# One MLP weight laid unevenly over the partitions, and part of it loaded early in small transfers

## The chip, the cores and the metric

The kernel runs on one core of a Trainium2 chip. The metric is the device time of one launch, in microseconds; the number for the kernel before is the median of three runs. Inside the launch, the profile's times count from the first instruction.

## The reference

One decode step of a transformer block whose norms are modulated by a condition vector. There is one token, D = 640, 32 heads of 192, a cache of 8192 positions, and an MLP of width 1536 with a squared ReLU. All is float32.

```python
mod = (silu(c) @ w_mod).reshape(1, 6, 1, -1)
sa, ca, ga, sb, cb, gb = (mod[:, i] for i in range(6))
h = layernorm(x) * (1 + ca) + sa
q = (h @ wq) per head
p = softmax(q . k_cache * 192 ** -0.5)
x = x + ga * ((p . v_cache) @ wo)
h = layernorm(x) * (1 + cb) + sb
h = relu(h @ w1 + b1)
x = x + gb * ((h * h) @ w2 + b2)
```

The caches are 2 x 32 x 8192 x 192 floats, about 403 MB, and every byte of them is read once.

## The kernel before

**Loads.** Everything big comes through one queue (SyncE, named SP), in the order in which the program writes the loads. A head has a load of keys (`load_k`, 48 KB per partition, and with them, for most heads, 7.5 KB of a query or output weight) and a load of values (`load_v`, 48 KB per partition). They go into a pool of three slots (`strm`, tag `slot`); a load waits on SP until its slot is free. All 128 partitions take part in each, with the same bytes. Behind head 31 come the weights of the tail, again through slots: `wm1` (last output weight and three modulation weights), `w1`, `gb`, and last `w2`, in the pieces of `W1_CUT` and `W2_CUT`.

**A head** (the loop over `h` near the end). `keys` multiplies the cached keys with the query on DVE (L201), adds the two halves of a part of the products on GpSimd (POOL, L203), and sums over the head dimension on DVE (L204, L205), in two halves of the positions, for the last head in four. `softmax` takes the maximum over partitions through TensorE (L220) and the exponential on ScalarE (L228). `values` multiplies with the cached values on TensorE (L240). `project` and `attend` turn a pair of heads into output rows a little later; `query` makes the next pair's query.

**The tail**, in this order: the last pair's `project` and `attend`, the second norm (with two modulation vectors made between its steps), the first MLP matmul `ps_f` (L343), bias, ReLU and square on DVE (L346 to L348), a transpose to columns (`fT`, L82), the last modulation vector (L140), two rounds of idle matmuls (L355), the second MLP matmul `ps_y` (L363), and two DVE operations (L366, L367) before the store of `y`.

**How the MLP lies on the partitions.** The 128 partitions are four groups of 32. The hidden width 1536 is cut into four parts of FG = 384, one per group, and each part into FB = 12 blocks of 32. The matmul `ps_f` therefore runs, for each of KB = 5 blocks of the input, four matmuls of 384 columns, one into each group's strip of output partitions. `fT` holds, per partition, one hidden element of each of the 12 blocks. `w2` is stored to match: each partition holds 12 rows of 640 floats, one per block, and `ps_y` runs 12 blocks of four matmuls of 160 columns over all 128 partitions. The load of `w2` is cut into pieces of 6, 3, 1, 1 and 1 blocks, and each piece's matmuls may start when it is there.

`spread` brings biases from columns to rows; its temporary tile and `f` share one buffer (tag `spread`).

Of the kernel before, what the change touches and what calls it, by code (L numbers as in the profile page):

```python
# [8 lines left out]
F32 = mybir.dt.float32  # L9
# [4 lines left out]
P = 128  # L14
D = 640
# [4 lines left out]
G = 4  # L20
DG = D // G
FG = FF // G
KB = DG // 32
FB = FG // 32
PW = 2 * DH
E = 8
ED = 64
# [9 lines left out]
WITHOUT_W = (1, H - 2)  # L37
WITH_W = tuple(h for h in range(H) if h not in WITHOUT_W)
W1_CUT = ((0, 3), (3, 2))
W2_CUT = ((0, 6), (6, 3), (9, 1), (10, 1), (11, 1))  # L40
WARM = 2
EPS = 1e-5


@with_exitstack
def block_kernel(ctx: ExitStack, tc: tile.TileContext, kw, ky, vc, wm0, wm1, w1, gb, w2, out):
    nc = tc.nc
    const = ctx.enter_context(tc.tile_pool(name="const", bufs=1))
    strm = ctx.enter_context(tc.tile_pool(name="strm", bufs=3))
    work = ctx.enter_context(tc.tile_pool(name="work", bufs=2))  # L50
# [3 lines left out]
    def slot(name):  # L54
        return strm.tile([P, SLOT], F32, tag="slot", name=name, bufs=3)
# [16 lines left out]
    wm0_t = slot("wm0_t")  # L72
    nc.sync.dma_start(wm0_t[:, :wm0.shape[1]], wm0)

    small = const.tile([P, 2 * KB + FB + KB], F32, name="small")
    nc.vector.tensor_copy(small, wm0_t[:, KB * 2 * D + WQ:wm0.shape[1]])  # L76
    x_c, c_c, bbc = small[:, :KB], small[:, KB:2 * KB], small[:, 2 * KB:]

    def columns(src, n, name, pool=const, **how):

        t = pool.tile([P, n // 32, 32], F32, name=name, **how)
        nc.vector.transpose(t.rearrange("p b r -> p (b r)"), src)  # L82
        return t

    def spread(src, n, name):

        t = work.tile([P, FB + KB, 32], F32, name=name + "_c", tag="spread", bufs=1)
        nc.vector.tensor_copy(t[:, :n], src[:, :, None].to_broadcast([P, n, 32]))
        r = const.tile([P, 32 * n], F32, name=name)
        nc.vector.transpose(r, t[:, :n].rearrange("p b r -> p (b r)"))  # L90
        return r
# [38 lines left out]
    mods = const.tile([P, 6, DG], F32, name="mods")  # L130
# [19 lines left out]
    def load(src, to, h, what):  # L150
        to[h] = slot(f"{what}{h}")
        n, w = CUTS.get((what, h), 1), src.shape[1]
        for c in range(n):
            a, b = c * HD // n, (c + 1) * HD // n if c + 1 < n else w
            nc.sync.dma_start(to[h][:, a:b], src[:, a:b])

    def load_k(h):

        load(kw[WITH_W.index(h)] if h in WITH_W else ky[WITHOUT_W.index(h)], k_t, h, "k")

    def load_v(h):
        load(vc[h], v_t, h, "v")
# [14 lines left out]
    def query(i, w):  # L177
        w = w.rearrange("p (b n) -> p b n", b=KB)
        ps = psum.tile([P, 512], F32, tag="q", name=f"ps_q{i}", bufs=2)
        for b in range(KB):  # L180
            nc.tensor.matmul(ps[:, :PW], hR[:, b], w[:, b], start=(b == 0), stop=(b == KB - 1))  # L181
        qb_t[i] = work.tile([P, PW], F32, name=f"qb{i}", tag="qb")
        nc.scalar.activation(qb_t[i], ps[:, :PW], AF.Copy, scale=DH ** -0.5)  # L183
# [27 lines left out]
    def inverse(i):  # L211
        r = work.tile([P, 2], F32, tag="r", name=f"r{i}")
        nc.vector.reciprocal(r, sum_t.pop(i))
        ri_t[i] = r
# [30 lines left out]
    def project(i):  # L245

        n = 32 * NV
        os_ = work.tile([P, 2, ED], F32, tag="os", name=f"os{i}")
        inverse(i)
        r2 = ri_t.pop(i)  # L250
        for a in range(2):
            h = 2 * i + a
            om = work.tile([P, ED, E], F32, tag="om", name=f"om{h}", bufs=1)
            nc.vector.scalar_tensor_tensor(om[:n], ps_t.pop(h)[:n].rearrange("p (d e) -> p d e", e=E), r2[:n, a:a + 1],  # L254
                                           mask[:n, None, :].to_broadcast([n, ED, E]), op0=ALU.mult, op1=ALU.mult)
            nc.vector.tensor_reduce(os_[:n, a], om[:n], axis=AX.X, op=ALU.add)  # L256
        os_t[i] = psum.tile([P, 512], F32, tag="sm", name=f"ps_oT{i}", bufs=2)
        nc.tensor.matmul(os_t[i][:, :n], os_[:n].rearrange("p a d -> p (a d)"), quad[:n], start=True, stop=True)

    def attend(i, w):  # L260
        oT = work.tile([P, 96], F32, tag="oT", name=f"oT{i}")
        nc.vector.tensor_copy(oT, os_t.pop(i)[:, :96])  # L262
        w = w.rearrange("p (j n) -> p j n", j=3)
        if i + 1 < NPAIR:
            for j in range(3):
                for g in range(2):
                    nc.tensor.matmul(att_a[32 * g:32 * (g + 1), :2 * DG], oT[:, 32 * j:32 * (j + 1)],  # L267
                                     w[:, j, 2 * DG * g:2 * DG * (g + 1)], start=(i == 0 and j == 0), stop=(i == NPAIR - 2 and j == 2))
            return
        for j in range(3):  # L270
            for g in range(G):
                nc.tensor.matmul(att_t[0][32 * g:32 * (g + 1), :DG], oT[:, 32 * j:32 * (j + 1)],
                                 w[:, j, DG * g:DG * (g + 1)], start=False, stop=(j == 2))

    def gather():

        nc.scalar.activation(att_s[:64], att_a[:64, :2 * DG], AF.Copy)
        att_t.append(psum.tile([P, 512], F32, tag="o", name="att", bufs=3))
        for g in range(G):
            nc.tensor.matmul(att_t[0][32 * g:32 * (g + 1), :DG], ident[:, 32 * (g // 2):32 * (g // 2) + 1].to_broadcast([P, 32]),  # L280
                             att_s[:, DG * (g % 2):DG * (g % 2 + 1)], start=True, stop=False)

    x_t = spread(x_c, KB, "x_t")
    bbt = spread(bbc, FB + KB, "bbt")
    for h in range(H):
        i = h // 2
        if h:
            load_k(h)
        if h == H - 1:
            wm1_t = slot("wm1_t")  # L290
            nc.sync.dma_start(wm1_t[:, :WO + KB * D], wm1[:, :WO + KB * D])
        load_v(h)
        w = k_t[h][:, HD:]

        def between(c):
            if c == 0 and h % 2 and i:
                attend(i - 1, w)
            elif c == 0 and h % 2 == 0 and i + 1 < NPAIR:
                query(i + 1, w)
            elif c == 2 and h == H - 1:  # L300
                gather()

        if h % 2 and i:
            project(i - 1)
        sc = keys(h, between)
        p = softmax(h, sc)
        if h == H - 1:
            next(mod(2, 1, wm1_t[:, WO:WO + KB * D].rearrange("p (b n) -> p b n", b=KB)))
        values(h, p)
# [3 lines left out]
    w1_t = slot("w1_t")  # L313
# [3 lines left out]
    w2_t = slot("w2_t")  # L317
    for b0, n in W2_CUT:
        nc.sync.dma_start(w2_t[:, b0 * D:(b0 + n) * D], w2[:, b0 * D:(b0 + n) * D])
    gb_t = w1_t[:, KB * FF:KB * (FF + D)].rearrange("p (b n) -> p b n", b=KB)  # L320
    w1_t = w1_t[:, :KB * FF].rearrange("p (b n) -> p b n", b=KB)
    w2_t = w2_t[:, :FB * D].rearrange("p (b n) -> p b n", b=FB)

    project(NPAIR - 1)
    attend(NPAIR - 1, wm1_t[:, :WO])
    mod_b = mod(3, 2, wm1_t[:, WO + KB * D:WO + KB * 3 * D].rearrange("p (b n) -> p b n", b=KB), (2, 2, 1))
# [11 lines left out]
    hT2 = columns(layernorm(x1, 32, scale_b, lambda: mods[:, 3], "ln2", lambda: next(mod_b)), DG, "hT2")  # L338

    pf = psum.tile([P, 512], F32, tag="q", name="ps_f", bufs=2)  # L340
    for b in range(KB):
        for g in range(G):
            nc.tensor.matmul(pf[32 * g:32 * (g + 1), :FG], hT2[:, b], w1_t[:, b, FG * g:FG * (g + 1)],  # L343
                             start=(b == 0), stop=(b == KB - 1))
    f = work.tile([P, FG], F32, name="f", tag="spread", bufs=1)
    nc.vector.tensor_add(f, pf[:, :FG], bbt[:, :FG])  # L346
    nc.vector.tensor_scalar(f, f, 0.0, None, op0=ALU.max)
    nc.vector.tensor_mul(f, f, f)  # L348
    fT = columns(f, FG, "fT", work, tag="om", bufs=1)

    next(mod(5, 1, gb_t))
    idle = psum.tile([P, 512], F32, tag="sm", name="ps_warm", bufs=2)
# [1 line left out]
        for g in range(G):  # L354
            nc.tensor.matmul(idle[32 * g:32 * (g + 1)], ones[:, :32], w1_t[:, k, :512], start=True, stop=True)  # L355
    gb2 = const.tile([P, DG], F32, name="gb2")
    nc.vector.tensor_mul(gb2, mods[:, 5], bbt[:, FG:])
    nc.vector.tensor_add(x1, x1, gb2)

    py = psum.tile([P, 512], F32, tag="q", name="ps_y", bufs=2)  # L360
    for b in range(FB):
        for g in range(G):
            nc.tensor.matmul(py[32 * g:32 * (g + 1), :DG], fT[:, b], w2_t[:, b, DG * g:DG * (g + 1)],  # L363
                             start=(b == 0), stop=(b == FB - 1))
    y = const.tile([P, DG], F32, name="y")
    nc.vector.tensor_mul(y, py[:, :DG], mods[:, 5])  # L366
    nc.vector.tensor_add(y, y, x1)  # L367
# [43 lines left out]
```

## Time and profile before

| | |
|---|---|
| median of three runs | 1057.88 us (1057.36 to 1058.01) |
| profiled execution, span | 1055.5 us |
| instructions | 5687 |
| DVE busy | 831.4 us (79%) |
| TensorE busy (PE) | 463.7 us (44%) |
| GpSimd busy (POOL) | 194.8 us (18%) |
| ScalarE busy (ACT) | 33.4 us (3%) |
| moved by DMA | 452.18 MB, mean 428 GB/s over the span |

The span runs from the first to the last instruction of the profiled execution; the median is 2.4 us above it, and that difference holds what lies around the instructions. A line such as "L201 DVE ... k<-k,qb" names the source line, the engine, the tile written and the tiles read. "Idle ... <-" is the time for which the engine stood still before the instruction, and what released it. "DMA share" is the mean busy share of the core's 16 DMA engines; q1 is the queue of the kernel's own loads, q8 and q14 bring instructions. The chain is followed back from the last instruction, at each step to what released it.

### The profile page before, as it was taken

To read this page: it belongs to the slowest core of one execution; us is meant where nothing else is said; L and a number is where in the kernel's file an instruction comes from. 1 tells how busy PE (TensorE), PEld (TensorE's weight loads), DVE (VectorE), ACT (ScalarE), POOL (GpSimd) and SP (SyncE) were. 2 spreads that over 40 slices of the span, in tenths; PEclk is the share of its full clock that TensorE was granted. 3 is DMA by queue.
4 is the path that set the end of the run, shared out by engine and by line. 5 is a ranking of instruction groups with operands and counts; after the bars stand their busy time and mean duration, and the time that the engine had idled before them with its cause. 6 is when DMAs were issued, how large, how long until landed. Compare 5 with 4: busy or idle time off the path is not lost.

```text
span 1055.5 us, 5687 instructions
## 1 busy us (share of the span) xinstructions
PE 463.7 (44%) x2356; PEld 155.0 (15%) x2356; DVE 831.4 (79%) x409; ACT 33.4 (3%) x88; POOL 194.8 (18%) x72
## 2 busy tenths in 40 slices
PE   3234443355543345463334534335453335535446
PEld 1101111111111111120111111101111111111113
DVE  2886878978787987878888687997878798789963
ACT  1000000000000000000000000000000000000000
POOL 0211112211212221212221212221221221122110
PEclk9667666766666766666676666666666666767769
DMA  9999999999999999999999999999999999999997
GB/s 403 435 434 428 432 440 427 441 424 437 433 433 428 440 424 441 424 439 427 431 437 437 422 442 430 428 439 426 439 429 433 428 438 433 434 427 432 424 426 310
DMA packets 11410, 452.18 MB, mean 428 GB/s; under 512 B 1269, under 2 KB 1273, under 8 KB 1785
## 3 DMA queue, kind: packets, MB, share of 16 engines
q1 hardware_dynamic: 11384, 451.83, 99.3%
q8 instruction: 18, 0.29, 0.1%
q14 instruction: 8, 0.06, 0.0%
HBM read 451.82 MB, written 0.00 MB: 428 GB/s over the span
## 4 chain that ended last, share of the span: by engine, by line
DMA 42%; DVE 39%; PE 17%; ACT 1%; issue 1%; SPq 0%; DVEq 0%; ACTq 0%
DMA k<-in_kw 36%; DVE k L201 21%; PE ps_o L240 14%; DVE sc L204 12%; DVE sc L205 5%; DMA k<-in_ky 3%; DMA w_t<-in_w 2%; PE ps_mx L220 1%; DMA wm_t<-in_wm 1%; ACT p L228 1%; PE ps_sum L97 1%; PE ps_mod L140 1%; PE ps_q L181 1%; DVE nm L222 0%; DVE mp L218 0%
## 5 line engine op out<-in xcount | busy, mean ns | idle before, releaser
L201 DVE TENSOR_TENSOR k<-k,qb 128x6144 f32<-128x6144 f32 (+1 forms) x66 | 419.7, 6359 | 141.6 <-DMA k<-in_kw 134.4
L203 POOL TENSOR_TENSOR k<-k 128x1344 f32<-128x1344 f32 (+1 forms) x66 | 194.1, 2941 | 820.9 <-DVE k L201 476.1
L240 PE MATMUL ps_o<-v,p 128*32 128x512 f32 x1536 | 290.4, 731 | 17.2 <-ACT p L228 17.2
L204 DVE TENSOR_REDUCE sc<-k 128x18 f32<-128x3456 f32 (+1 forms) x66 | 240.5, 3644 | 4.3
L220 PE MATMUL ps_mx<-ident,mp 128*128 128x128 f32 x64 | 25.5, 501 | 416.2 <-DVE mp L218 416.2
L240 PEld LDWEIGHTS ps_o<-v,p 128*32 128x32 f32 x1536 | 68.4, 131 | 215.4 <-issue 193.1
L267 PE MATMUL att_a<-k,oT 128*32 128x320 f32 x180 | 49.6, 720 | 114.2 <-DVE oT L262 113.1
L205 DVE TENSOR_REDUCE sc<-k 128x14 f32<-128x1344 f32 (+1 forms) x66 | 99.0, 1500 | 0.0
L220 PEld LDWEIGHTS ps_mx<-ident,mp 128*128 128x128 f32 x64 | 16.1, 312 | 442.8 <-DVE mp L218 421.0
L181 PE MATMUL ps_q<-k,hR 128*128 128x384 f32 x150 | 52.3, 496 | 0.0
L228 ACT ACTIVATE p<-sc,nm 128x256 f32<-128x256 f32 x32 | 16.2, 508 | 760.6 <-DVE nm L222 496.9
L267 PEld LDWEIGHTS att_a<-k,oT 128*32 128x32 f32 x180 | 13.7, 161 | 136.7 <-DVE oT L262 116.7
L222 DVE TENSOR_REDUCE nm<-ps_mx 128x1 f32<-128x128 f32 x32 | 9.3, 291 | 28.5 <-PE ps_mx L220 28.5
L181 PEld LDWEIGHTS ps_q<-k,hR 128*128 128x128 f32 x150 | 27.3, 190 | 27.9 <-issue 11.7
L254 DVE SCALAR_TENSOR_TENSOR om<-ps_o,r,mask 96x512 f32<-96x512 f32 x32 | 23.9, 747 | 6.5 <-PE ps_o L240 5.4
L256 DVE TENSOR_REDUCE os<-om 96x64 f32<-96x512 f32 x32 | 21.8, 682 | 1.1
L140 PE MATMUL ps_mod<-wm_t,silu 128*32 128x320 f32 (+1 forms) x120 | 11.7, 550 | 14.6 <-DVE silu L128 14.6
L97 PE MATMUL ps_sum<-sp,ones 128*128 128x2 f32 x32 | 9.4, 364 | 17.2 <-ACT p L228 17.2
L183 ACT ACTIVATE qb<-ps_q 128x384 f32<-128x384 f32 x16 | 7.9, 491 | 195.2 <-PE ps_q L181 195.2
L97 PEld LDWEIGHTS ps_sum<-sp,ones 128*128 128x128 f32 x32 | 8.0, 312 | 21.9 <-ACT p L228 21.9
L145 DVE COPY mods<-ps_mod 128x320 f32<-128x320 f32 (+1 forms) x4 | 1.6, 398 | 10.2 <-PE ps_mod L140 10.2
L76 DVE COPY small<-wm_t 128x27 f32<-128x27 f32 x1 | 0.2, 179 | 11.2 <-DMA wm_t<-in_wm 11.2
(77 smaller groups left out, 90.9 us busy)
## 6 DMA issues: line engine op xcount, KB each, us to landing
k<-in_kw SPq DMA_DIRECT2D x29, 7104.0 KB, 27.4
v<-in_vc SPq DMA_DIRECT2D x32, 6144.0 KB, 22.1
k<-in_ky SPq DMA_DIRECT2D x1, 6144.0 KB, 28.3
k<-in_ky SPq DMA_DIRECT2D x2, 3072.0 KB, 21.5
k<-in_kw SPq DMA_DIRECT2D x3, 1536.0 KB, 15.5
wm_t<-in_wm SPq DMA_DIRECT2D x1, 4173.5 KB, 12.7
wm_t<-in_wm SPq DMA_DIRECT2D x1, 3200.0 KB, 29.3
wm_t<-in_wm SPq DMA_DIRECT2D x1, 2560.0 KB, 18.2
```

What stands on the lines that cost most here:

```text
L97: nc.tensor.matmul(ps[:, :n], ones, src, start=True, stop=True)
L140: nc.tensor.matmul(ps[32 * g:32 * (g + 1), :n * DG], e[:, b:b + 1].to_broadcast([P, 32]), wb[:, :, DG * g:DG * (g + 1)], start=(b == 0), s ...
L181: nc.tensor.matmul(ps[:, :PW], hR[:, b], w[:, b], start=(b == 0), stop=(b == KB - 1))
L201: nc.vector.tensor_mul(pr, pr, q[:, None, :].to_broadcast([P, n, DH]))
L203: nc.gpsimd.tensor_add(half, half, pr[:, m:, DH // 2:])
L204: nc.vector.tensor_reduce(s[:, :m], pr[:, :m], axis=AX.X, op=ALU.add)
L205: nc.vector.tensor_reduce(s[:, m:], half, axis=AX.X, op=ALU.add)
L220: nc.tensor.matmul(ps[:, :P], mp.to_broadcast([P, P]), ident, start=True, stop=True)
L228: nc.scalar.activation(p, sc[:, :, None].to_broadcast([P, NPOS, 32 // E]), AF.Exp, bias=nm, accum_out=sp[:, h % 2:h % 2 + 1])
L240: nc.tensor.matmul(ps_t[h][32 * g:32 * (g + 1)], p[:, E * j:E * (j + 1)].rearrange("p e r -> p (e r)"), t[:, j, g], start=(j == 0), stop=( ...
L254: nc.vector.scalar_tensor_tensor(om[:n], ps_t.pop(h)[:n].rearrange("p (d e) -> p d e", e=E), r2[:n, a:a + 1], mask[:n, None, :].to_broadca ...
L267: nc.tensor.matmul(att_a[32 * g:32 * (g + 1), :2 * DG], oT[:, 32 * j:32 * (j + 1)], w[:, j, 2 * DG * g:2 * DG * (g + 1)], start=(i == 0 an ...
```

## The change

The four groups no longer hold equal parts of the hidden width. Groups 0 and 1 (partitions 0 to 63) hold 14 blocks of 32, groups 2 and 3 (partitions 64 to 127) hold 10. The sum is 1536 as before.

- The load `w2`, last in the program, has 10 blocks for all 128 partitions, in pieces of 5, 2, 1, 1 and 1.
- The four blocks that only partitions 0 to 63 have, 64 rows of 10,240 B, 655 KB in all, go into a tile of their own, `w2x_t`. They come in eight transfers of eight rows each, issued by SP behind the values' load of heads 8, 10, 12, 14, 16, 18, 20 and 22. One transfer takes every fourth of 32 consecutive partitions: rows r, r+4, ... r+28.
- `ps_f` has matmuls of 448, 448, 320 and 320 columns in place of four of 384.
- `f` is 448 wide. Its last 128 columns are zeroed on partitions 64 to 127 before the last `project`. The bias is added in two operations: 320 columns on all partitions, 128 columns on partitions 0 to 63. The ReLU, the square and the transpose are 448 wide.
- `ps_y` runs 14 blocks: first the four of `w2x_t`, over 64 partitions, then the ten of `w2`.
- The bias columns in the first load grow by two per partition.

```diff
-FB = FG // 32
+FB = 10
+FX = 4
+FT = FB + FX
+F0 = (0, 32 * FT, 64 * FT, 64 * FT + 32 * FB)
+FN = (32 * FT, 32 * FT, 32 * FB, 32 * FB)
...
-W2_CUT = ((0, 6), (6, 3), (9, 1), (10, 1), (11, 1))
+W2_CUT = ((0, 5), (5, 2), (7, 1), (8, 1), (9, 1))
+X_AT = {8 + 2 * r: (r % 4) + 32 * (r // 4) for r in range(8)}
...
+    w2x_t = const.tile([64, FX * D], F32, name="w2x_t")
     for h in range(H):
...
         load_v(h)
+        if h in X_AT:
+            r = X_AT[h]
+            top = 32 * (r // 32 + 1)
+            nc.sync.dma_start(w2x_t[r:top:4], w2x[r:top:4])
...
+    f = work.tile([P, 32 * FT], F32, name="f", tag="spread", bufs=1)
+    nc.vector.memset(f[64:, 32 * FB:], 0.0)
     project(NPAIR - 1)
...
-            nc.tensor.matmul(pf[32 * g:32 * (g + 1), :FG], hT2[:, b], w1_t[:, b, FG * g:FG * (g + 1)],
+            nc.tensor.matmul(pf[32 * g:32 * (g + 1), :FN[g]], hT2[:, b], w1_t[:, b, F0[g]:F0[g] + FN[g]],
                              start=(b == 0), stop=(b == KB - 1))
-    f = work.tile([P, FG], F32, name="f", tag="spread", bufs=1)
-    nc.vector.tensor_add(f, pf[:, :FG], bbt[:, :FG])
+    nc.vector.tensor_add(f[:, :32 * FB], pf[:, :32 * FB], bbt[:, :32 * FB])
+    nc.vector.tensor_add(f[:64, 32 * FB:], pf[:64, 32 * FB:32 * FT], bbt[:64, 32 * FB:32 * FT])
     nc.vector.tensor_scalar(f, f, 0.0, None, op0=ALU.max)
     nc.vector.tensor_mul(f, f, f)
-    fT = columns(f, FG, "fT", work, tag="om", bufs=1)
+    fT = columns(f, 32 * FT, "fT", work, tag="om", bufs=1)
...
+    w2x_b = w2x_t.rearrange("p (b n) -> p b n", b=FX)
+    for b in range(FX):
+        for g in range(G):
+            nc.tensor.matmul(py[32 * g:32 * (g + 1), :DG], fT[:64, FB + b], w2x_b[:, b, DG * g:DG * (g + 1)],
+                             start=(b == 0), stop=False)
     for b in range(FB):
         for g in range(G):
             nc.tensor.matmul(py[32 * g:32 * (g + 1), :DG], fT[:, b], w2_t[:, b, DG * g:DG * (g + 1)],
-                             start=(b == 0), stop=(b == FB - 1))
+                             start=False, stop=(b == FB - 1))
```

The arrays are laid out to match on the host: `w2` as [128, 10 x 640], `w2x` as [64, 4 x 640].

More of the change, by code (lines that the diff above doesn't have):

```diff
@@ L45, in block_kernel @@
 @with_exitstack
-def block_kernel(ctx: ExitStack, tc: tile.TileContext, kw, ky, vc, wm0, wm1, w1, gb, w2, out):
+def block_kernel(ctx: ExitStack, tc: tile.TileContext, kw, ky, vc, wm0, wm1, w1, gb, w2, w2x, out):
     nc = tc.nc
@@ L73, in block_kernel @@
     nc.sync.dma_start(wm0_t[:, :wm0.shape[1]], wm0)
-    small = const.tile([P, 2 * KB + FB + KB], F32, name="small")
+    small = const.tile([P, 2 * KB + FT + KB], F32, name="small")
     nc.vector.tensor_copy(small, wm0_t[:, KB * 2 * D + WQ:wm0.shape[1]])
@@ L85, in spread @@
     def spread(src, n, name):
-        t = work.tile([P, FB + KB, 32], F32, name=name + "_c", tag="spread", bufs=1)
+        t = work.tile([P, FT + KB, 32], F32, name=name + "_c", tag="spread", bufs=1)
         nc.vector.tensor_copy(t[:, :n], src[:, :, None].to_broadcast([P, n, 32]))
@@ L283, in block_kernel @@
     x_t = spread(x_c, KB, "x_t")
-    bbt = spread(bbc, FB + KB, "bbt")
+    bbt = spread(bbc, FT + KB, "bbt")
+    w2x_t = const.tile([64, FX * D], F32, name="w2x_t")
     for h in range(H):
@@ L356, in block_kernel @@
     gb2 = const.tile([P, DG], F32, name="gb2")
-    nc.vector.tensor_mul(gb2, mods[:, 5], bbt[:, FG:])
+    nc.vector.tensor_mul(gb2, mods[:, 5], bbt[:, 32 * FT:])
     nc.vector.tensor_add(x1, x1, gb2)
     py = psum.tile([P, 512], F32, tag="q", name="ps_y", bufs=2)
+    w2x_b = w2x_t.rearrange("p (b n) -> p b n", b=FX)
[3 more added lines that the diff above has]
+                             start=(b == 0), stop=False)
     for b in range(FB):
@@ L385, in column, with hidden @@
         return a(v).reshape(G, n, 32).transpose(0, 2, 1).reshape(P, n)
+    def hidden(v):
+        b = np.zeros((P, FT), np.float32)
+        for g in range(G):
+            b[32 * g:32 * (g + 1), :FN[g] // 32] = a(v)[F0[g]:F0[g] + FN[g]].reshape(-1, 32).T
+        return b
+    w2 = a(B_w2)
+    w2m = np.stack([w2[F0[g]:F0[g] + 32 * FB].reshape(FB, 32, D).transpose(1, 0, 2) for g in range(G)])
+    w2e = np.stack([w2[F0[g] + 32 * FB:F0[g] + 32 * FT].reshape(FX, 32, D).transpose(1, 0, 2) for g in range(2)])
     wq = a(A_wq).reshape(G, KB, 32, NPAIR, PW).transpose(3, 0, 2, 1, 4).reshape(NPAIR, P, WQ)
@@ L397 @@
         "wm0": np.concatenate([rows(wm[:, :2 * D], KB), wq[0], column(A_x, KB), column(c, KB),
-                               column(B_b1, FB), column(B_b2, KB)], axis=1),
+                               hidden(B_b1), column(B_b2, KB)], axis=1),
         "wm1": np.concatenate([wo[-1], rows(wm[:, 2 * D:3 * D], KB), rows(wm[:, 3 * D:5 * D], KB)], axis=1),
@@ L401 @@
         "gb": rows(wm[:, 5 * D:], KB),
-        "w2": rows(B_w2, FB),
+        "w2": np.ascontiguousarray(w2m.reshape(P, FB * D)),
+        "w2x": np.ascontiguousarray(w2e.reshape(64, FX * D)),
     }
```

## The prediction

> **What bounds the kernel now.** I read the page first, for the engines, the DMA line and the chain.
>
> ```profile
> span 1055.5 us, 5687 instructions
> DMA  9999999999999999999999999999999999999997
> q1 hardware_dynamic: 11384, 451.83, 99.3%
> q8 instruction: 18, 0.29, 0.1%
> DMA 42%; DVE 39%; PE 17%; ACT 1%; issue 1%; SPq 0%; DVEq 0%; ACTq 0%
> ```
>
> The loads fill the 16 DMA engines for the whole span, apart from the last slice. DVE has the second largest share of the chain. So for each stage I ask which of the two ends last. The chain in order of time answers that for the end of the program.
>
> ```profile
> 912.48 26.83 DMA k<-in_kw
> 939.40 6.57 DVE k L201
> 963.46 0.81 PE ps_mx L220 x2
> 964.50 6.56 DVE k L201
> 1022.94 7.32 PE ps_o L240 x48
> 1032.07 19.60 DMA w_t<-in_w
> 1051.71 0.52 PE ps_y L363 x8
> ```
>
> The keys of head 29 (L201 at 939.40) are the last work of DVE that waits for a load. From there up to the last values (L240 at 1022.94) the chain shows DVE at heads 29, 30 and 31, with little but a short PE step between heads. Windows of this stretch say the same (columns: window, length, busy PE, PEld, DVE, ACT, POOL, clock, DMA share, GB/s):
>
> ```profile
> 965.00:975.00 10.00, 9.13 (x50) 2.54 (x50) 9.90 (x3) 0.28 (x2) 3.06 (x1) 0.80 1.01 437
> 1005.00:1015.00 10.00, 0.00 (x0) 0.00 (x0) 9.93 (x6) 0.00 (x0) 1.93 (x2) 0.58 1.02 437
> ```
>
> DVE is busy for 9.9 of 10 us. What follows (last values, attention output, norm, MLP) hangs on it. There are thus two paths to the end. One is compute, started by the landing of head 29's keys. The other is w2 itself, whose last piece the chain names. They end close together, as the timeline of the tail shows:
>
> ```profile
> 1039.47 5.13 PE L343 MATMUL ps_f<-w_t,hT 128*32 128x384 f32 x40 [2.10 <-issue]
> 1044.38 1.57 PE L140 MATMUL ps_mod<-w_t,silu 128*32 128x160 f32 x40
> 1045.74 1.93 PE L355 MATMUL ps_warm<-w_t,ones 128*32 128x512 f32 x16
> 1046.23 0.58 DVE L82 STREAM_TRANSPOSE fT<-f 128x384 f32<-128x384 f32 x1
> 1047.46 3.16 PE L363 MATMUL ps_y<-w_t,fT 128*32 128x160 f32 x80
> 1050.92 0.48 PE L363 MATMUL ps_y<-w_t,fT 128*32 128x160 f32 x8 [0.31 <-DMA w_t<-in_w]
> 1051.71 0.48 PE L363 MATMUL ps_y<-w_t,fT 128*32 128x160 f32 x8 [0.31 <-DMA w_t<-in_w]
> ```
>
> From 1047.46 to 1052.19 PE idles only twice for 0.31 us on w2, so the wait that can be removed here is 0.6 us.
>
> **Are the 16 engines alike?** The change moves bytes from one half of the partitions to the other, so this decides. Windows at the end of the loads:
>
> ```profile
> 1046.00:1047.00 1.00, 1.00 (x12) 0.32 (x8) 0.96 (x3) 0.00 (x0) 0.00 (x0) 1.00 0.98 392
> 1047.00:1048.00 1.00, 1.00 (x25) 0.70 (x20) 0.67 (x3) 0.00 (x0) 0.00 (x0) 1.00 0.60 241
> 1048.00:1049.00 1.00, 1.00 (x39) 0.98 (x31) 0.00 (x0) 0.00 (x0) 0.00 (x0) 1.00 0.58 221
> 1049.00:1050.00 1.00, 0.98 (x31) 0.66 (x24) 0.00 (x0) 0.00 (x0) 0.00 (x0) 1.00 0.54 197
> 1049.80:1050.00 0.20, 0.20 (x12) 0.19 (x8) 0.00 (x0) 0.00 (x0) 0.00 (x0) 1.00 0.40 154
> 1051.20:1051.40 0.20, 0.20 (x8) 0.00 (x0) 0.00 (x0) 0.00 (x0) 0.00 (x0) 1.00 0.00 0
> ```
>
> They are not. The share stands at 0.60 to 0.54, which is nine engines of 16 (0.56). Seven are done by about 1047, the nine between 1049.8 and 1051.2. So every engine had the same bytes, seven are early by some 3 us, and nine are late, spread over at most 1.4 us. A cause shows in a window around one packet of the instruction queue, and in the window up to head 29's keys:
>
> ```profile
> q8 instruction: 1, 0.02, 6.0%
> DMA packets 8690, 405.69 MB, mean 432 GB/s; under 512 B 961, under 2 KB 961, under 8 KB 961
> q1 hardware_dynamic: 8669, 405.41, 100.0%
> q8 instruction: 14, 0.23, 0.1%
> ```
>
> The first line is from a window of 1.0 us: 6.0% of 16 us is 0.96 us of one engine for one block of instructions. Fourteen of the 18 have come by 939.4, so the unevenness is mostly there by head 29. At 100.0% no engine idles before that: what an engine is given on top delays everything behind it in its queue.
>
> **The change, part by part.**
>
> *The eight transfers of eight rows.* Each row has 4 x 640 x 4 = 10,240 B. An engine moves 432/16 = 27.0 GB/s, so a row takes 0.38 us. How eight rows fall on engines the trace of before does not show. The nearest row is the output, four rows:
>
> ```profile
> DMA packets 8, 0.00 MB, mean 1 GB/s; under 512 B 4, under 2 KB 8, under 8 KB 8
> ```
>
> This window holds only that store: four rows, four completion writes (under 512 B), so four engines with a row each. I take eight engines with a row each, the same eight each time: 8 x 0.38 = 3.03 us on each of them, all before head 23, none on the other eight. Only seven engines are early. Whichever eight they are, at least one is of the nine late ones, and DVE starts head 29 when the last engine has landed its part. That engine is now later by 3.03 us, less what it was ahead of the latest of the nine (0 to 1.4 us). So the keys of head 29 land later by 1.6 to 3.0 us. I take 2.4, the middle, and all compute behind 939.40 moves with it.
>
> [...]
>
> SP issues each transfer behind the values' load of its head, into a tile of its own, so it waits for no slot; the issue holds up only the next key load, which waits for its slot anyway. Cost taken: nothing; bound 0.1 us each, off the path while engines never run dry.
>
> *w2 shorter by two blocks, all 128 rows.* Every engine saves 8 x 2 x 2560 B = 40,960 B, or 1.52 us, in the tail. Late engines outside the eight end w2 1.5 us earlier; the eight end 1.5 us later net. What is worth having is only the 0.6 us of PE waits.
>
> *The first MLP matmul.* Groups of 448, 448, 320, 320 columns replace four of 384. The four sit in different column strips and run side by side, so the longest should set the pace: 5.13 x 448/384 = 5.98, that is +0.85 us. Below: 0, if the sum of columns (1536 as before) counts. I take +0.85. The next two PE groups (L140, L355) follow at once and move with it.
>
> *DVE between the matmuls.* Rows for 384 columns and 160 columns:
>
> ```profile
> 1044.65 0.56 DVE L346 TENSOR_TENSOR f<-ps_f,bbt 128x384 f32<-128x384 f32 x1 [5.29 <-PE ps_f L343]
> 1045.24 0.36 DVE L347 TENSOR_SCALAR f<-f 128x384 f32<-128x384 f32 x1
> 1045.64 0.56 DVE L348 TENSOR_TENSOR f<-f 128x384 f32<-128x384 f32 x1
> 1033.69 0.33 DVE L329 TENSOR_TENSOR x<-att,mods 128x160 f32<-128x160 f32 x1 [1.15 <-PE att L272]
> 1037.96 0.24 DVE L335 TENSOR_SCALAR cb<-mods 128x160 f32<-128x160 f32 x1
> ```
>
> An add costs 0.23/224 us, about 1.0 ns, per column. One add of 384 becomes one of 320 and one of 128: 0.49 + 0.30 against 0.56, +0.23. The clamp gains 64 columns at 0.5 ns (+0.03), the square and the transpose 64 at 1.0 ns each (+0.13). Sum +0.39. fT is then ready 0.85 + 0.39 = 1.24 us after its 1046.81, at 1048.05; ps_y started 0.65 us after fT, held by the warm-up, which began at 1045.74 and took 1.93. It now starts between 1047.46 + 0.85 = 1048.3 (the warm-up's shift) and 1048.05 + 0.65 = 1048.7. I take 1048.45, +1.0.
>
> *The second MLP matmul.* 14 blocks for 12, the extra ones on half of the rows. The same shape without waits is L140's, here with its mean:
>
> ```profile
> L140 PE MATMUL ps_mod<-w_t,silu 128*32 128x160 f32 x40 | 1.6, 299 | 0.0
> ```
>
> Its 40 are ten steps of four side by side, in 1.57 us: (1.57 - 0.30)/9 = 0.141 us a step. A block of w2 is two steps, 14 blocks take 27 x 0.141 + 0.30 = 4.1 us (4.4 at an undivided 1.57/5 a block), if w2 is there. They end at 1052.55 against 1052.19: +0.36 us. Bounds: 0, if the columns' sum counts (the first matmul then costs nothing), and +0.9, with 4.4 us and a slower clock in the first matmul.
>
> *Zeroing f's unused half, wider bias, two columns more in the first load.* The memset runs on DVE before it waits for the last values, and there is cover:
>
> ```profile
> L254 DVE SCALAR_TENSOR_TENSOR om<-ps_o,r,mask 96x512 f32<-96x512 f32 x32 | 23.9, 747 | 6.5 <-PE ps_o L240 5.4
> ```
>
> 5.4 us of idle DVE hide some 0.2 us, which would be the price without it. The bias work stands before the first keys land. Cost: nothing.
>
> **Sum.** Head 29's keys +2.4, tail +0.36, together +2.75 us. Is w2 late instead? Before, its last piece freed PE at 1051.71; an engine of the eight ends 1.5 us later, at 1053.2 or earlier, while compute now wants the last blocks at about 1052.5 + 2.4. So compute ends last and w2 is off the path. The profiled execution's span would be 1055.5 + 2.75 = 1058.2; it stands 2.4 us under the median of 1057.88, so the median should be 1060.6. Bounds of this case: 1.6 + 0 gives 1059.5, 3.0 + 0.9 gives 1061.8.
>
> **The rivals.** *Not slower.* The eight engines hold the seven early ones and one that is late only at the very end (four of 18 instruction blocks come behind head 29's keys). If at head 29 it is within half a microsecond or so of the early ones (the 3 to 4 us from them to the latest, less 3.03), the 3.03 us stay inside the others' lateness, the path moves by nothing, the PE waits of 0.6 us go, and the tail gives +0.36 or, if the matmul follows the sum of columns, 1047.46 + 0.39 + 4.1 = 1051.95, -0.24 us. Time 1057.6 to 1058.3. For it: the windows show lateness at the end only. Against: 14 of 18 blocks were there before. The point is that half microsecond.
>
> *The rows do not fall on eight engines but on all 16, by halves or in turn.* Then each gets 1.52 us, head 29's keys are 1.5 late, and the time is 1057.88 + 1.5 + 0.36 = 1059.8. Against: the four writes of the output.
>
> *All eight rows on one engine, the same each time.* 8 x 8 x 0.38 = 24 us on it, of which up to 3 are its lead: 1079 to 1082. The change would not do what it says. Against: again four writes for four rows.
>
> [...]
>
> **How the numbers follow.** The main case gets 0.72; not slower 0.14; all 16 engines 0.06; one engine 0.03; fixed price 0.03; 0.02 for something unseen that gains. About 0.2% (2.1 us, from 1057.88 to 1060.0) is what a measurement of this kernel can tell from no change. The main case lies at 1059.5 to 1061.8, so about a sixth of it (0.12) is within 0.2%. Slower: 0.60 + 0.03 + 0.03 = 0.66; within: 0.12 + 0.13 + 0.06 = 0.31; faster 0.03. The likeliest is the main case, 1060.6. Range: its bounds, and down to 1058.1 to take in most of the not-slower case: 1058.1 to 1061.9.
>
> **What would show it.** Right: DVE's first keys of head 29 start near 941.8 rather than 939.40, and L363 starts near 1050.9 and runs 14 blocks without a DMA wait; L343 takes near 6.0 us; the windows at the end show the two groups of engines closer together and one or more of the eight last. Wrong: L201 for head 29 at 939.4 to 939.9 (then no engine's lateness grew), or a chain that still ends in a wait for w2. [...]

## The result, and the profile after

The kernel after takes 1059.68 us (median of 20 runs, 1058.53 to 1060.37), the kernel before beside it 1057.7 us: 1.0019 times as long, 95% interval 1.0012 to 1.0025. It is slower by 2.0 us (1.3 to 2.6), where 2.75 was forecast. A difference of 0.2% lies inside the interval: the point, 0.19%, belongs to what the forecast called within 0.2% (chance 0.31), the upper part of the interval to slower by more (0.66).

The page of after, the lines that answer to those of before:

```profile
span 1057.4 us, 5730 instructions
DMA  9999999999999999999999999999999999999996
q1 hardware_dynamic: 11512, 451.83, 99.1%
q8 instruction: 18, 0.29, 0.1%
DMA 40%; DVE 39%; PE 19%; ACT 1%; issue 1%; DVEq 0%; ACTq 0%
```

The chain in order of time (start, length, what):

```profile
915.73 26.15 DMA k<-in_kw
941.98 6.57 DVE k L206
966.04 0.81 PE ps_mx L225 x2
967.08 6.56 DVE k L206
992.83 9.05 PE ps_o L245 x48
1026.20 7.66 PE ps_o L245 x48
1051.33 2.90 PE ps_y L380 x80
```

Head 29's keys start on DVE at 941.98, not 939.40: 2.58 us later. Head 30's keys follow at the same distance; from its values (`ps_o` at 992.83) on it is more, of which below. The chain no longer ends in a load of w2; it ends in the second MLP matmul, which waits for no load. The timeline of the tail:

```profile
1043.08 3.58 PE L355 MATMUL ps_f<-w_t,hT 128*32 128x448 f32 x38 [2.10 <-issue]
1046.46 0.57 PE L355 MATMUL ps_f<-w_t,hT 128*32 128x448 f32 x2
1047.10 0.49 DVE L357 TENSOR_TENSOR f<-ps_f,bbt 128x320 f32<-128x320 f32 x1 [4.12 <-PE ps_f L355]
1047.51 0.27 DVE L358 TENSOR_TENSOR f<-ps_f,bbt 64x128 f32<-64x128 f32 x1
1048.90 0.65 DVE L87 STREAM_TRANSPOSE fT<-f 128x448 f32<-128x448 f32 x1
1050.04 1.29 PE L376 MATMUL ps_y<-w2x_t,fT 64*32 64x160 f32 x32
1051.26 2.92 PE L380 MATMUL ps_y<-w_t,fT 128*32 128x160 f32 x80
```

ps_y ends at 1054.18, before at 1052.19: 1.99 us later, which is the whole loss (the spans differ by 1.9). The engines at the end of the loads, in windows as before:

```profile
1047.00:1048.00 1.00, 1.00 (x37) 1.00 (x34) 0.86 (x3) 0.00 (x0) 0.00 (x0) 1.00 1.00 387
1048.00:1049.00 1.00, 1.00 (x20) 0.71 (x16) 0.93 (x3) 0.00 (x0) 0.00 (x0) 1.00 0.68 266
1049.00:1050.00 1.00, 1.00 (x12) 0.14 (x2) 0.97 (x3) 0.00 (x0) 0.00 (x0) 1.00 0.31 123
1050.00:1051.00 1.00, 1.00 (x30) 0.91 (x32) 0.44 (x2) 0.00 (x0) 0.00 (x0) 1.00 0.25 88
```

The step at nine engines is gone. Most now finish within a microsecond or two of each other, but four (0.25) are later still. The layout did even out most of the engines. The last of them no longer hold up PE; what costs is that three engines are late at head 29 (their landings are below).

### The profile page after: what moved, and what is told of

The parts are those of the page before. It is cut to its first block, busy times and chain, and to the rows that moved or that the text cites. A ratio compares the mean times of both kernels' runs of the same rounds, so it can differ in the third digit from the quotient of the medians.

```text
span 1057.4 us, 5730 instructions
## 1 busy us (share of the span) xinstructions
PE 466.2 (44%) x2372; PEld 155.6 (15%) x2372; DVE 832.1 (79%) x411; ACT 33.4 (3%) x88; POOL 194.8 (18%) x72
## 4 chain that ended last, share of the span: by engine, by line
DMA 40%; DVE 39%; PE 19%; ACT 1%; issue 1%; DVEq 0%; ACTq 0%
DMA k<-in_kw 36%; DVE k L206 21%; PE ps_o L245 14%; DVE sc L209 12%; DVE sc L210 5%; DMA k<-in_ky 3%; PE ps_mx L225 1%; DMA wm_t<-in_wm 1%; PE ps_mod L145 1%; ACT p L233 1%; PE ps_sum L102 1%; PE ps_q L186 0%; DVE nm L227 0%; DVE mp L223 0%; PE ps_f L355 0%
## 5 line engine op out<-in xcount | busy, mean ns | idle before, releaser
L245 PE MATMUL ps_o<-v,p 128*32 128x512 f32 x1536 | 296.7, 744 | 17.2 <-ACT p L233 17.2
```

What stands on the lines that cost most here:

```text
L245: nc.tensor.matmul(ps_t[h][32 * g:32 * (g + 1)], p[:, E * j:E * (j + 1)].rearrange("p e r -> p (e r)"), t[:, j, g], start=(j == 0), stop=( ...
```

## The experiments

Each ran beside the kernel before, on the same chip. "Head 29" is the start of the first half of that head's keys on DVE (L201; 939.40 before). Where a diff takes out lines of the transfers, it is against the first of these kernels, the transfers alone; in the last three experiments it is against the kernel after. Lines that only make the tile and its array are left out, and `...` marks other cuts.

**The transfers alone** (the MLP and w2 as before).

```diff
+        if h in X_AT:
+            r = X_AT[h]
+            top = 32 * (r // 32 + 1)
+            nc.sync.dma_start(w2x_t[r:top:4], w2x[r:top:4])
```

> The kernel before, with only the eight transfers of eight rows added (655 KB into a tile that nothing reads; w2 and the MLP as before). Theory (the last of the eight engines to land a head's keys sets the pace): head 29's keys start on DVE near 942.0, as after the change, against 939.4, and the whole time is 2.3 to 3.0 us above the kernel before. Rival (the time of the change comes from the uneven MLP in the tail, the transfers are hidden): head 29 at 939.4 to 939.9 and the time within 0.5 us of before. Rival (only bytes count): +1.5 us.

1060.11 us, 1.0023 (1.0014 to 1.0032), 2.6 us over before's 1057.55. Head 29, on the timeline of DVE:

```profile
941.92 6.56 DVE L202 TENSOR_TENSOR k<-k,qb 128x6144 f32<-128x6144 f32 x1 [3.25 <-DMA k<-in_kw]
```

This is the change's delay at head 29, without its MLP: the transfers are not hidden. The end of the chain differs from that of after, though:

```profile
1035.52 18.52 DMA w_t<-in_w
1054.08 0.52 PE ps_y L369 x8
```

With w2 at its full length, its last piece frees PE at 1054.08, 2.37 us later than before. The late engines thus delay both paths, and here w2 is the one that ends last. The change shortens w2, which leaves the path through head 29. That the uneven MLP is not what costs is worked out below, from the timeline of after.

**The same bytes over all 16 engines.**

```diff
+            r, b = X_AT[h]
+            nc.sync.dma_start(w2x_t[r::4, b * D:(b + 1) * D], w2x[r::4, b * D:(b + 1) * D])
```

> The kernel before, with the same 655 KB added at the same eight heads, but over all 128 partitions: eight transfers of 32 rows of 2,560 B, two rows on each of 16 engines. Not read. Theory: each engine gets 1.5 us instead of eight getting 3.0, so head 29's keys start near 940.9 and the time is 1.3 to 1.7 us above before. Rival (a fixed price per transfer, wherever it goes): as much as the transfers to 64 partitions. Rival (hidden): 0 to 0.5.

1059.13 us, 1.0015 (1.0006 to 1.0024), 1.6 us; head 29:

```profile
941.19 6.56 DVE L202 TENSOR_TENSOR k<-k,qb 128x6144 f32<-128x6144 f32 x1 [3.24 <-DMA k<-in_kw]
```

That is 1.79 us, near the 1.5 of an even share. At most 0.3 us is left for a fixed price of all eight transfers.

**Twice over to partitions 0 to 63**, one transfer at each of heads 8 to 23.

```diff
-X_AT = {8 + 2 * r: (r % 4) + 32 * (r // 4) for r in range(8)}
+X_AT = {8 + r: (r % 4) + 32 * (r // 4 % 2) for r in range(16)}
```

> The kernel before, with the eight transfers of eight rows to partitions 0 to 63 made twice over, one at each of heads 8 to 23 (1.3 MB, not read). Theory: 6.1 us on each of the eight engines in place of 3.0, all of the second 3.0 unhidden: head 29's keys at 944.9 to 945.2, the time 5.4 to 5.9 us above before. Rival (a part is hidden, or the price is paid once): 2.5 to 4 us.

1062.84 us, 1.0050 (1.0035 to 1.0066), 5.2 us; head 29:

```profile
945.29 6.56 DVE L202 TENSOR_TENSOR k<-k,qb 128x6144 f32<-128x6144 f32 x1 [3.25 <-DMA k<-in_kw]
```

The time lies under the 5.4 to 5.9 of the theory and over the 2.5 to 4 of the rival; head 29, at 945.29, is just past the theory's 945.2. The second set adds 3.37 us to head 29 after the first added 2.52: the second pays in full (3.0 by bytes), the first had a little hidden. In time the second set costs no more than the first (5.2 is twice 2.6), so this run does not tell the theory from a price by bytes.

**Four rows instead of eight**, half the bytes.

```diff
-            nc.sync.dma_start(w2x_t[r:top:4], w2x[r:top:4])
+            nc.sync.dma_start(w2x_t[r:r + 16:4], w2x[r:r + 16:4])
```

> The kernel before, with eight transfers of four rows of 10,240 B (rows r, r+4, r+8, r+12; half of the bytes of the transfers-only run), not read. Theory (3.0 us on each of the four lowest of the eight engines): it depends on whether one of the three late ones is among the four. If so, head 29's keys at 941.9 to 942.1 and 2.2 to 2.8 us above before, as with twice the bytes; if not, head 29's keys at 939.4 to 940.0 and 0 to 0.7 us. Rival (bytes count): 0.7 us for four engines' share, or half of 2.6, 1.3 us, with head 29's keys near 940.7.

1059.39 us, 1.0016 (1.0007 to 1.0025), 1.5 us, less than the 2.2 foretold for this case; but head 29 agrees with it:

```profile
941.72 6.56 DVE L202 TENSOR_TENSOR k<-k,qb 128x6144 f32<-128x6144 f32 x1 [3.23 <-DMA k<-in_kw]
```

Half the bytes, on four engines, delay the keys by 2.32 us, nearly as eight rows do. In the trace's completion marks of these keys, 15 engines have landed by 939.63 and one at 941.63. In the kernel after, 13 have landed by 939.39 and three at 941.5 to 941.9. Before, the marks are in two groups: seven engines at 935.71 to 936.44, nine at 937.70 to 939.31. So for the landing of the keys the one late engine counts, not the bytes. The time of the whole, 1.5 us, is nearer the rival's 1.3 than the theory's 2.2 to 2.8; why it is less than the keys' delay is open.

**Fewer TensorE instructions** (the values' matmul over one of its eight blocks of positions; the other seven are left out, the loads stay).

```diff
-        for j in range(n):
+        for j in range(n // 8):
...
-                                 t[:, j, g], start=(j == 0), stop=(j == n - 1))
+                                 t[:, j, g], start=(j == 0), stop=(j == n // 8 - 1))
```

> The kernel before, with the values' matmul (L240) over the first of its eight blocks of positions only: seven eighths of that matmul's work and instructions are left out, all loads stay. Theory (nine engines are late because they also bring the instructions, most of them TensorE's): the instruction queue q8 moves some 7 packets in place of 18, the late engines are less late, head 29's keys start 0.5 to 1.5 us earlier than 939.4 and the time falls by as much or more. Rival (the engines differ by themselves): the same two groups at the end of the loads, head 29 at 939.2 to 939.6.

1056.6 us, 0.9991 (0.9982 to 1.0000), 1.05 us under before; head 29 at 938.85, 0.55 earlier. The queue of instructions on its page, and the end of the loads:

```profile
q8 instruction: 8, 0.13, 0.1%
...
1047.00:1048.00 1.00, 1.00 (x37) 0.99 (x31) 0.00 (x0) 0.00 (x0) 0.00 (x0) 1.00 0.51 202
1048.00:1049.00 1.00, 0.62 (x22) 0.30 (x15) 0.00 (x0) 0.00 (x0) 0.00 (x0) 1.00 0.33 124
1049.00:1050.00 1.00, 0.98 (x32) 0.58 (x20) 0.00 (x0) 0.00 (x0) 0.00 (x0) 1.00 0.06 26
```

Eight blocks in place of 18, and the shares at the end fall at once (0.51, 0.33, 0.06) where they stood at 0.60, 0.58, 0.54. Up to head 29's keys it is five blocks of q8 in place of 14, and the landing marks of these keys show ten engines at 935.46 to 936.37 and six at 937.03 to 938.76, where seven were early and nine late. Lateness goes with the instructions that are brought; the last engine gains little, 0.55 us. This kernel does less matmul work too, so its time alone would prove little; the shares and the landings are the evidence. Which engine brings which block no view names.

**The other half.** The same eight rows, to partitions 64 to 127.

```diff
-            nc.sync.dma_start(w2x_t[r:top:4], w2x[r:top:4])
+            nc.sync.dma_start(w2x_t[64 + r:64 + top:4], w2x[r:top:4])
```

> The kernel before, with the eight transfers of eight rows into partitions 64 to 127 in place of 0 to 63. Not read. Theory (nine of 16 engines are late, so either half holds late ones): head 29's keys start at 941.9 to 942.5, the time is 2.3 to 3.1 us above before. Rival (one half holds the early engines and the change picked the wrong one): here the transfers are hidden, head 29 at 939.4 to 939.9 and at most 0.5 us above before.

1065.88 us, 1.0076 (1.0064 to 1.0089), 8.3 us. Both theories missed: at most 3.1 had a place in mine. Head 29:

```profile
947.76 6.56 DVE L202 TENSOR_TENSOR k<-k,qb 128x6144 f32<-128x6144 f32 x1 [3.23 <-DMA k<-in_kw]
```

A window over all eight transfers, 285 to 745, shows what is different (last two columns: DMA share, GB/s); transfers to 0 to 63 first, then to 64 to 127:

```profile
285.00:745.00 460.00, 196.96 (x892) 63.57 (x890) 375.04 (x160) 12.33 (x36) 90.80 (x30) 0.68 1.00 433
```

```profile
285.00:745.00 460.00, 195.96 (x892) 63.38 (x892) 369.90 (x158) 12.33 (x36) 87.76 (x29) 0.68 1.00 427
```

The engines are busy all the time in both, but the second moves 427 GB/s, not 433 (before: 432): over 460 us, 6.4 us of work is missing. The trace's records of single DMA packets show where. A row of 56,832 B of the key loads takes 2.1 us. In this window one of 1896 such rows takes over 15% longer before, one of 1888 with the transfers to 0 to 63, and 103 of 1840 with those to 64 to 127. Over all rows of the key and value loads, the time above the median row adds up to 106 us, against 13 with the transfers to 0 to 63: 5.8 us more on each of 16 engines. So the transfers get in the way of the rows of other loads.

**Both halves, 16 rows**, to see whether the upper half stays dear when as many rows go to the lower.

```diff
+            nc.sync.dma_start(w2x_t[r::8], w2x[r::8])
```

> The kernel before, with eight transfers of 16 rows of 10,240 B, eight rows of partitions 0 to 63 and eight of 64 to 127 in each: twice the bytes (1.3 MB), not read. [...] Rival (rows to partitions 64 to 127 are dear whoever carries them): 8 us or more above before.

1070.59 us, 1.0123 (1.0109 to 1.0137), 12.9 us; 424 GB/s in the same window; head 29:

```profile
953.28 6.56 DVE L202 TENSOR_TENSOR k<-k,qb 128x6144 f32<-128x6144 f32 x1 [3.24 <-DMA k<-in_kw]
```

This is what the rival said. I had expected 942.3 to 942.6 and 2.8 to 3.3 us, by a guess at which engine writes which rows; the run went against it, and no view names a row's engine. The rival (the upper half is dear) was still alive, so the next run keeps to the lower half.

**Neighbouring rows in the lower half.** Bytes, rows, count and half are those of the first run.

```diff
-            nc.sync.dma_start(w2x_t[r:top:4], w2x[r:top:4])
+            nc.sync.dma_start(w2x_t[r:r + 8], w2x[r:r + 8])
```

> The kernel before, with eight transfers of eight rows of 10,240 B to partitions 0 to 63 as in the transfers-only run, but each to eight neighbouring partitions (8r to 8r+7) in place of every fourth. Not read. [...] Rival (rows to partitions 64 to 127 are dear, those to 0 to 63 are not): head 29's keys at 942.0, 2.3 to 2.9 us above before.

1067.11 us, 1.0091 (1.0076 to 1.0106), 9.3 us, against 2.6 with every fourth row. Head 29, and the window:

```profile
949.66 6.56 DVE L202 TENSOR_TENSOR k<-k,qb 128x6144 f32<-128x6144 f32 x1 [3.24 <-DMA k<-in_kw]
...
285.00:745.00 460.00, 196.45 (x895) 63.51 (x892) 369.16 (x158) 12.34 (x36) 87.77 (x29) 0.67 1.00 427
```

In this window 100 of 1838 rows of 56,832 B take over 15% longer, where it was one of 1888 with every fourth partition. The rival's 942.0 is out; I had expected 946 or later and 7 us or more, and that came. So the half alone does not decide: neighbours in the lower half are as dear (9.3 us) as every fourth partition in the upper (8.3). Within one half, which partitions the rows of one transfer go to does (9.3 us against 2.6). That such a transfer slows the rows of other loads is shown; the reason is not, since no view names a packet's engine.

**The transfers moved behind head 29's keys**, in three ways, with the uneven MLP.

```diff
-X_AT = {8 + 2 * r: (r % 4) + 32 * (r // 4) for r in range(8)}
+X_AT = (0, 1, 2, 3, 32, 33, 34, 35)
+X_HEAD = 29
...
-        if h in X_AT:
-            r = X_AT[h]
...
+        if h == X_HEAD:
+            for r in X_AT:
...
```

> The kernel after, with the eight transfers issued together right behind the values' load of head 29, so that head 29's keys are not behind them. Theory: head 29's keys start at 939.4 as before the change; what is left of the change is the uneven MLP and up to 1 us from the last values or the last MLP weights on late engines: 1057.3 to 1059.0, at least 1 us under the kernel after. Rival (the uneven MLP costs the time): as slow as after, 1059.5 or more.

```diff
-X_AT = {8 + 2 * r: (r % 4) + 32 * (r // 4) for r in range(8)}
+X_AT = (0, 1, 2, 3, 32, 33, 34, 35)
...
-        if h in X_AT:
-            r = X_AT[h]
...
+    for r in X_AT:
+        top = 32 * (r // 32 + 1)
+        nc.sync.dma_start(w2x_t[r:top:4], w2x[r:top:4])
     w2_t = slot("w2_t")
```

> The kernel after, with the eight transfers issued at the end, right ahead of w2, so that no head and no earlier weight is behind them. Theory: head 29's keys at 939.4 as before; now w2 ends last on the late ones of the eight engines, 1.5 us later than before: the time is 0.6 to 1.6 us above before and under the kernel after. Rival (the tail's matmuls are what costs): the end is not a wait for w2, and the time is 1.5 us or more above before. Rival (the uneven layout gains once the keys are left alone): faster than before by 0.3 us or more.

Behind head 29: 1061.0 us, 1.0031 (1.0019 to 1.0043), head 29 at 939.50. Ahead of w2: 1060.83 us, 1.0029 (1.0019 to 1.0040), head 29 at 939.50. The keys are free in both, yet neither is under the kernel after: 3.4 and 3.2 us over before by the medians, where after has 2.0 (the intervals overlap). Two misses. The waits of SP in each say why:

```profile
SPq L303 <- DMA v<-in_vc: 13.9, 1, 13.9
SPq L303 <- DMA k<-in_kw: 3.1, 1, 3.1
```

```profile
SPq L325 <- DMA w_t<-in_w: 9.4, 2, 4.9
SPq L325 <- DMA wm_t<-in_wm: 6.7, 1, 6.7
SPq L325 <- DMA w_t<-in_gb: 3.0, 1, 3.0
```

L303 and L325 are the transfers. SP held them until earlier loads had landed, 17 and 19 us in all, and what is queued behind waits too. (The trace of the first is its fastest execution, 1.7 us under its median.) In the second, the DMA engines ran dry just before w2 (window 1042 to 1044, share 0.09) and PE waited 3.3 us for w2:

```profile
1042.00:1044.00 2.00, 2.00 (x32) 1.07 (x30) 0.08 (x1) 0.00 (x0) 0.00 (x0) 1.00 0.09 36
...
PE ps_y L379 <- DMA w_t<-in_w: 3.3, 1, 3.3
```

My reading is that eight loads issued in a row use up the marks by which loads tell that they have landed: in the traces of before and after these marks (1269 and 1341) lie on eight semaphores. So I tried four and four:

```diff
-X_AT = {8 + 2 * r: (r % 4) + 32 * (r // 4) for r in range(8)}
+X_AT = {29: (0, 1, 2, 3), 30: (32, 33, 34, 35)}
...
-        if h in X_AT:
-            r = X_AT[h]
+        for r in X_AT.get(h, ()):
```

> The kernel after, with four of the eight transfers issued behind the values' load of head 29 and four behind that of head 30, so that SP need not wait for a completion mark to come free before it can issue them, as it did when all eight stood together. Theory: head 29's keys start at 939.4; the late ones among the eight engines bring head 31's values and the tail's weights later by up to 2.6 us, of which the work before them hides 1.5 or more; 0.3 to 1.6 us above before and under the kernel after. Rival (what is left is the uneven MLP's price): 1.7 us or more above before.

1058.39 us, 1.0007 (0.9998 to 1.0016): 0.5 us over before, not to be told from it, and head 29 at 939.86. With the same bytes, layout and MLP as the kernel after, the place of the transfers alone gives 1.5 of the 2.0 us back by the medians (0.5 with -0.2 to 1.7, against 2.0 with 1.3 to 2.6). It does not beat the kernel before. No run pointed to a version that would.

## Why the prediction was right

**Which term is it.** Head 29's keys were to be 1.6 to 3.0 us late, 2.4 taken (the middle of the bounds is 2.3). After: 2.58; the transfers alone: 2.52. The landing marks show the reason given, that the latest engine among those that carry rows sets the landing: three marks stand 2.1 us or more behind the other 13. The four-row run speaks against "bytes count": half the bytes moved head 29 by 2.32, not 1.3. Of the term's 8 x 0.38, the row holds: 0.39 us in the trace of after. Eight engines with a row each agree with eight marks a transfer: in the window 285 to 745 the transfers alone have 528 packets under 512 B, before has 464. That they are the same eight each time no run shows; what the runs show is 2.52 us at head 29 for the first set and 3.37 more for the second.

The number alone would not have shown this. Rows over all 16 engines, a rival, was to give 1059.8, and the measured 1059.68 is nearer to that than to the main case's 1060.6. Head 29 decides: 941.98, where 1.5 us would be 940.9.

**Seven early, so one late in any eight.** The argument held. It was read from the end of the loads, and the landing marks show the same seven and nine at head 29. In fact three late engines are among the eight.

**The tail, +0.36.** This term was mis-sized. From head 29 to the end of ps_y, after gains 0.59 us on before (1.99 less 2.58). ps_y itself came out as worked out: 14 blocks in 4.14 us (forecast 4.1), without a wait for a load. DVE's two adds took 0.49 and 0.27 (forecast 0.49 and 0.30). What I had wrong is the clock of ps_f. The windows over it, before and after:

```profile
1039.40:1044.60 5.20, 5.13 (x48) 2.45 (x52) 0.00 (x0) 0.00 (x0) 0.00 (x0) 0.67 1.01 428
```

```profile
1043.00:1047.00 4.00, 3.92 (x49) 2.11 (x53) 0.00 (x0) 0.00 (x0) 0.00 (x0) 1.00 0.99 407
```

It ran at 0.67 of the clock before and at 1.00 after. I scaled 5.13 us to 5.98; it took 3.95, so the sign "L343 near 6.0" failed. The scaling itself was sound: at full clock, 384 columns take 3.43 us in the run with the transfers alone,

```profile
1042.92 3.43 PE L349 MATMUL ps_f<-w_t,hT 128*32 128x384 f32 x40 [2.09 <-issue]
```

and 448 take 3.95, +15% for +17% columns. Against this gain of 1.2 us stand 1.0 us that after loses between head 29 and ps_f (2.58 late at 941.98, 3.61 late at 1043.08). The values' matmul of heads 30 and 31 on the chain was shorter before:

```profile
990.26 8.36 PE ps_o L240 x48
1022.94 7.32 PE ps_o L240 x48
```

After has 9.05 and 7.66, with the same work; over these stretches the granted clock was 0.84 and 0.95 before, 0.78 and 0.91 after. The forecast had neither effect of the clock, and that they nearly cancel is luck. At one clock the uneven tail would come out even, by an estimate from these rows: +0.52 for ps_f (3.95 against 3.43), +0.31 on DVE, -0.16 between fT and ps_y (0.49 against 0.65) and -0.59 for ps_y are +0.08 us. Whether the granted clock differs in just this way in every execution is not settled: ps_f ran at 1.00 in the traces of all eleven experiments as well, and at 0.67 only in the one trace of before. The medians moved by as much as the profiled executions did (2.0 and 1.9).

**w2 off the path.** Right: L380 shows no wait for a load, and the chain no longer passes through w2.

**The rivals.** Rows over all 16 engines: out by head 29, 941.19 in the run that does this and 941.98 after; the times, 1.6 and 2.0, would not have told. One engine carrying all: out, by the size. A fixed price for each transfer: no run shows one; the even run's eight cost 1.6 us in all, and at head 29 at most 0.3 us is left beside the bytes. Nor does a run show the bound of 0.1 us for an issue: SP took 0.65 us for each of the eight in after, off the path. Not slower: out; its condition, that the late engine among the eight is within half a microsecond of the early ones at head 29, did not hold.

## What to carry to other kernels

Here all DMA engines were busy from end to end (share 1.00 in the window 285 to 745), and bytes moved to the front were not hidden: they shifted the landing of head 29's keys by 2.52 us, by the forecast's reading what the latest engine among the carriers gets (3.03), less its lead over the last. Before giving one part of the partitions more, read from the share at the end of the loads how many engines are early, and whether the part that you would load holds only such. Put extra loads behind the last load for which compute waits, and not many in a row: four behind the values of head 29 and four behind those of head 30 left 0.5 us over before, all eight in a row behind those of head 29 left 3.4, and one each at eight heads from 8 to 22 left 2.0. Mind which partitions the rows of a small transfer go to: every fourth of 0 to 63 cost 2.6 us here, neighbours 9.3.

## What the hardware showed that I had not expected

Eight transfers of eight rows of 10 KB cost 2.6 us in all when they go to every fourth partition of 0 to 63, 9.3 when they go to eight neighbours, 8.3 when they go to every fourth of 64 to 127: in the two dear cases the DMA engines stay at a share of 1.00 and fall from 433 to 427 GB/s, while some hundred rows of other loads take over 15% longer. Lateness goes with the instructions that are brought: with eight blocks of instructions in place of 18, six engines in place of nine land head 29's keys late, and the last loads end sooner. And a run of eight small loads stopped SP for 17 to 19 us.
